# Projection weights and a weight remainder moved from the SyncE load queue to the ScalarE load queue, with a staging buffer

## The chip, the cores and the metric

The kernel runs on one core of one Trainium2 chip. The metric is device time in microseconds (us), the median over several executions. Ratios are the mean time of one kernel's runs over the mean of the other's in the same rounds, so they are not quite the ratio of the medians that are quoted.

## The reference, cut to what matters

The program adds three things: the input `x` (8 rows of 640), an attention block over a key and value cache, and a small MLP. Attention has 8 batch rows, 32 heads, 4096 cached positions and a head size of 128, in bfloat16.

```python
xn = layernorm(x)
q = xn @ wq                                    # wq 640 x 4096
p = softmax(q . k_cache / sqrt(128))           # k_cache 8 x 32 x 4096 x 128
o = p . v_cache                                # v_cache the same size
out = x + o @ wo + mlp(xn)                     # wo 4096 x 640; mlp: w1 640 x 1728, w2 1728 x 640
```

K and V together are 537 MB (8 x 32 x 4096 x 128 elements, 2 bytes, twice), read once. The weights are 15 MB: wq and wo 5.2 MB each, w1 and w2 2.2 MB each.

## The kernel before

The work is cut into 64 tiles. A tile is one batch row and a "quad" of four heads: 4 MB of K (32 KB in each of 128 partitions) and 4 MB of V. Eight tiles make a quad, and each quad needs its own 0.66 MB slice of `wo`. There are two K buffers and two V buffers. Each operation carries a position; operations of one engine run in order of position, and waits follow from what they read (`R`) and write (`W`). Tile `t` has its scores near position `t`, its values near `t + 2`. Repeated windows of operations become hardware loops.

All large loads are issued by SyncE, which does nothing else, in one queue:

```python
def ld(pos, dst, src, W, sem, R=()):
    add("sp", pos, lambda e: e.dma_start(dst, src() if callable(src) else src), R=R, W=W, sem=sem)
...
# K of tile t at t - 1.5, V of tile t at t + 0.6 (the first two of each earlier)
ld(-95.1, w2_sb[:, 0:FC, :], ..., ["w2"], "w2")
ld(-95.0, w2_sb[0:FR, FC, :], B_w2[FC * P:F, :], ["w2r"], "w2r")
for hg in range(NG):                                # NG = 8 quads, B = 8 tiles each
    ld(hg * B + 3.65, wo_sb[:, :, :],
       lambda hg=hg: A_wo[span(hg, HT * P), :].rearrange("(a p) n -> p a n", p=P), ["wo"], "wo")
```

The projection of the previous quad's last pair of tiles reads `wo_sb` at position 3.33 of the quad, so the load at 3.65 has to wait for it, and every K and V load behind it in the queue waits as well:

```python
def pe_o(e):
    for a in range(HT):
        for c in range(DC):
            r = e.matmul(ACC_ps[:, c * B:(c + 1) * B], wo_sb[:, a, c * P:(c + 1) * P], oTn_sb[:, a, :], ...)
add("pe", g * GT + 5.33 ..., pe_o, R=["wo", "oTn"], W=["ACC"], X=["ACC"], sig=True)
```

VectorE computes three quarters of the scores (a product, an add, a reduction, twice per tile, 17 us in all); TensorE does the other quarter and the value sums.

## Time and profile before

| | before |
|---|---|
| time, median of 3 | 1293.12 us (1292.88 to 1293.37) |
| moved by DMA | 552.00 MB |
| VectorE / TensorE / ScalarE busy | 1122.2 / 640.8 / 497.1 us of 1291.2 |

Parts 2 and 3 of the page of the kernel before: the mean busy share of the 16 DMA engines and their rate, in 40 slices of 32.3 us, and the queue that SyncE issues on, with packets, MB and share of 16 engines' span.

```profile
DMA  9999999999999999999999999999999999999997
GB/s 407 423 427 427 435 429 431 433 429 427 434 430 431 428 434 427 434 431 427 430 434 430 432 427 431 430 434 430 427 432 431 431 433 428 429 432 430 429 435 329
q1 hardware_dynamic: 23472, 551.80, 99.7%
```

The engines that move data are busy for 90% or more of every slice but the last. The DMA part of the page of the same kernel gives for each load the count, the size and the median time from issue to landing:

```profile
KV_sb<-in_A_k_cache_dram SPq DMA_DIRECT2D x64, 4096.0 KB, 26.8
KV_sb<-in_A_v_cache_dram SPq DMA_DIRECT2D x63, 4096.0 KB, 35.2
wo_sb<-in_A_wo_dram SPq DMA_DIRECT2D x8, 640.0 KB, 30.9
```

At 431 GB/s, 4 MB take 9.7 us. A load that lands 27 to 35 us after its issue has therefore stood behind two or three others: there is a backlog. The waits of the SyncE queue itself, in the kernel before (who, on whom: us in total, times, longest):

```profile
SPq L178 <- DVE Y_sb L544: 948.9, 56, 20.7
SPq L365 <- PE PV_ps L616: 75.6, 50, 20.8
SPq L365 <- PE ACC_ps L676: 43.5, 8, 6.2
```

The first two are waits for a K or V buffer to come free, the normal way in which consumers pace a full stream. The third is what the change is aimed at: 43.5 us in which the queue stood before the eight wo loads. Last, three links of the chain that ended last (start, length, what), before:

```profile
247.17 35.06 DMA KV_sb<-in_A_v_cache_dram
285.91 36.95 DMA KV_sb<-in_A_v_cache_dram
326.54 35.17 DMA KV_sb<-in_A_v_cache_dram
```

A link is one V load from issue to landing. The landings are at 282.23, 322.86 and 361.71 us. Two tiles of K and V lie between two of them: 38.85 us without a wo load, 40.63 us with one. So a wo load costs some 1.77 us of the stream.

VectorE's costliest group before (busy, mean ns of one, idle just before it and what ended it) shows that VectorE waits for data:

```profile
L544 DVE TENSOR_TENSOR Y_sb<-KV_sb,qbc_sb 128x6144 bf16<-128x6144 bf16 x128 | 429.1, 3353 | 91.0 <-DMA KV_sb<-in_A_k_cache_dram 76.4
```

### The profile page before, as it was taken

The page shows a single profiled execution, that of the slowest core. Times are in us where ns is not written, and L with a number is a line of the kernel's source. Part 1 is how long each engine was busy: PE and PEld are TensorE (multiplying, and loading weights), DVE is VectorE, ACT ScalarE, POOL GpSimd, SP SyncE. Part 2 cuts the span into 40 slices and gives each one's busy share as a digit, 9 for nine tenths or more (in the row PEclk, how much of TensorE's full clock was granted, in tenths as well). Part 3 has the DMA queues.
Part 4 walks back from the last instruction along what each step waited for, and adds up shares of the span by engine and source line. Part 5 has one row for each costly group of instructions (what it writes and reads, how often), then busy time and mean ns, then how long its engine had stood idle before and what let it go on. Part 6 is the DMA issues. An engine that isn't in the chain of part 4 may idle for free.

```text
span 1291.2 us, 19910 instructions
## 1 busy us (share of the span) xinstructions
PE 640.8 (50%) x7958; PEld 406.5 (31%) x7960; DVE 1122.2 (87%) x586; ACT 497.1 (39%) x1244; POOL 0.2 (0%) x4
## 2 busy tenths in 40 slices
PE   2754455444554454454455445545544554544555
PEld 1433233323333233233233233333332332322332
DVE  4989999898898898898988988988888988889885
ACT  1444344324344334344244342343442443433442
POOL 0000000000000000000000000000000000000000
PEclk9755655565555565655655555555555655556556
DMA  9999999999999999999999999999999999999997
GB/s 407 423 427 427 435 429 431 433 429 427 434 430 431 428 434 427 434 431 427 430 434 430 432 427 431 430 434 430 427 432 431 431 433 428 429 432 430 429 435 329
DMA packets 23520, 552.00 MB, mean 428 GB/s; under 512 B 2297, under 2 KB 6481, under 8 KB 6482
## 3 DMA queue, kind: packets, MB, share of 16 engines
q1 hardware_dynamic: 23472, 551.80, 99.7%
q8 instruction: 8, 0.13, 0.0%
q14 instruction: 6, 0.05, 0.0%
q10 hardware_dynamic: 34, 0.02, 0.0%
HBM read 551.80 MB, written 0.01 MB: 427 GB/s over the span
## 4 chain that ended last, share of the span: by engine, by line
DMA 83%; PE 8%; DVE 7%; issue 2%; ACT 0%; SPq 0%; DVEq 0%
DMA KV_sb<-in_A_v_cache_dram 78%; PE PV_ps L616 8%; DVE Y_sb L544 4%; DMA KV_sb<-in_A_k_cache_dram 2%; DMA KV_sb<-in_A_wq_dram 2%; DVE Y_sb L548 2%; DVE S_sb L551 1%; SPq L365 0%; PE PV_ps L626 0%; DVE M_sb L563 0%; PE CH_ps L565 0%; PE TR_ps L665 0%; PE TR_ps L456 0%; PE CH_ps L478 0%; DVE rinv_sb L597 0%
## 5 line engine op out<-in xcount | busy, mean ns | idle before, releaser
L544 DVE TENSOR_TENSOR Y_sb<-KV_sb,qbc_sb 128x6144 bf16<-128x6144 bf16 x128 | 429.1, 3353 | 91.0 <-DMA KV_sb<-in_A_k_cache_dram 76.4
L551 DVE TENSOR_REDUCE S_sb<-Y_sb 128x48 f32<-128x3072 bf16 x128 | 429.2, 3353 | 4.4
L515 ACT ACTIVATE KT_sb<-TR_ps 128x1024 bf16<-128x1024 bf16 x256 | 254.6, 1021 | 229.2 <-PE TR_ps L512 227.8
L616 PE MATMUL PV_ps<-KV_sb,P_sb 128*16 128x512 bf16 x2040 | 223.1, 616 | 144.2 <-DMA KV_sb<-in_A_v_cache_dram 144.2
L512 PE MATMUL TR_ps<-ident_bf,KV_sb 128*128 128x128 bf16 x2048 | 248.4, 308 | 74.7 <-DMA KV_sb<-in_A_k_cache_dram 74.7
L548 DVE TENSOR_TENSOR Y_sb<-Y_sb 128x3072 bf16<-128x3072 bf16 x128 | 225.0, 1758 | 4.4
L512 PEld LDWEIGHTS TR_ps<-ident_bf,KV_sb 128*128 128x128 bf16 x2048 | 200.4, 141 | 85.1 <-DMA KV_sb<-in_A_k_cache_dram 79.3
L522 PE MATMUL S_ps<-qk_sb,KT_sb 128*128 128x4 bf16 x2048 | 98.0, 170 | 135.7 <-ACT KT_sb L515 133.9
L635 ACT ACTIVATE E_sb<-PV_ps 128x512 bf16<-128x512 f32 (+1 forms) x65 | 38.5, 592 | 320.7 <-PE PV_ps L616 318.8
L616 PEld LDWEIGHTS PV_ps<-KV_sb,P_sb 128*16 128x16 bf16 x2040 | 62.5, 124 | 256.9 <-DMA KV_sb<-in_A_v_cache_dram 149.6
L522 PEld LDWEIGHTS S_ps<-qk_sb,KT_sb 128*128 128x128 bf16 x2048 | 85.9, 109 | 167.1 <-ACT KT_sb L515 167.1
L583 ACT ACTIVATE P_sb<-S_sb,NB_sb 32x128 bf16<-32x128 f32 x256 | 101.9, 398 | 3.8
L641 PE MATMUL C_ps<-sel_bf,E_sb 128*128 128x4 bf16 x256 | 16.9, 172 | 137.9 <-DVE rinv_sb L597 114.8
L577 ACT ACTIVATE NB_sb<-CH_ps 128x2 f32<-128x2 f32 (+1 forms) x33 | 5.7, 172 | 171.1 <-PE CH_ps L573 171.1
L565 PE MATMUL CH_ps<-ident_f,M_sb 128*2 128x128 f32 (+1 forms) x33 | 12.1, 366 | 114.1 <-DVE M_sb L563 114.1
L641 PEld LDWEIGHTS C_ps<-sel_bf,E_sb 128*128 128x128 bf16 x256 | 11.4, 103 | 167.9 <-DVE rinv_sb L597 114.1
L532 ACT ACTIVATE S_sb<-S_ps 32x32 f32<-32x32 f32 x256 | 48.3, 189 | 32.0 <-PE S_ps L522 29.8
L583 ACT ACTIVATION_READ_ACCUMULATOR P_sb<-S_sb,NB_sb 32x1 f32 x256 | 47.1, 184 | 0.0
L565 PEld LDWEIGHTS CH_ps<-ident_f,M_sb 128*2 128x2 f32 (+1 forms) x33 | 2.6, 80 | 117.1 <-DVE M_sb L563 117.1
L656 DVE MEMSET oTn_sb<- 128x16 uint32 x31 | 2.2, 72 | 31.1 <-PE ACC_ps L676 31.1
L567 DVE TENSOR_REDUCE M_sb<-CH_ps 2x4 f32<-2x128 f32 (+1 forms) x33 | 9.2, 279 | 15.1 <-PE CH_ps L565 15.1
L676 PE MATMUL ACC_ps<-oTn_sb,wo_sb 128*128 128x8 bf16 x620 | 21.5, 169 | 0.0
(93 smaller groups left out, 196.1 us busy)
## 6 DMA issues: line engine op xcount, KB each, us to landing
KV_sb<-in_A_k_cache_dram SPq DMA_DIRECT2D x64, 4096.0 KB, 26.8
KV_sb<-in_A_v_cache_dram SPq DMA_DIRECT2D x63, 4096.0 KB, 35.2
KV_sb<-in_A_wq_dram SPq DMA_DIRECT2D x1, 5120.0 KB, 24.0
wo_sb<-in_A_wo_dram SPq DMA_DIRECT2D x8, 640.0 KB, 30.9
KV_sb<-in_B_w_dram SPq DMA_DIRECT2D x1, 2160.0 KB, 39.2
w_sb<-in_B_w_dram SPq DMA_DIRECT2D x1, 2080.0 KB, 43.8
KV_sb<-in_A_v_cache_dram SPq DMA_DIRECT2D x1, 2048.0 KB, 12.6
KV_sb<-in_A_v_cache_dram SPq DMA_DIRECT2D x2, 1024.0 KB, 15.3
```

Of the source, the lines that this page charges most:

```text
L512: r = e.transpose(TR_ps[:, it.box[0], jj * P:(jj + 1) * P], kv[:, n * BK + jj, :], ident_bf[:, :])
L515: add("act", t - 0.59 + 0.12 * n, lambda e: e.activation(KT_sb[:, m % NS, :, :].rearrange("p a b -> p (a b)"), TR_ps[:, it.box[0], :], ACT ...
L522: r = e.matmul(S_ps[:, c:c + HT], KT_sb[:, m % NS, jj, :], qk_sb[:, :, i], start=True, stop=True)
L532: r = e.activation(S_sb[s, g % SR, i, 0:JP], S_ps[s, 0:JP * HT].rearrange("p (j a) -> p j a", a=HT)[:, :, a], ACT.Copy)
L544: return e.tensor_tensor(y, kv[:, j0:j1, :], qbc_sb[:, g % 2, i, :][:, None, :].to_broadcast([P, nj, P]), ALU.mult)
L548: lambda e, y=y, y2=y2: e.tensor_tensor(y2, y[:, :, 0:P // 2], y[:, :, P // 2:P], ALU.add),
L551: lambda e, y2=y2, j0=j0, j1=j1: e.tensor_reduce(S_sb[:, g % SR, i, j0:j1], y2, AX.X, ALU.add),
L583: r = e.activation(P_sb[s, i, :, a, :], S_sb[s, g % SR, i, :].rearrange("p (m c) -> p m c", c=4), ACT.Exp, bias=NB_sb[s, g % 2, i:i + 1], ...
L616: r = e.matmul(PV_ps[32 * ct:32 * ct + HT * 4, t % 2, :], P_sb[:, i, m, :, :].rearrange("p a c -> p (a c)"), vv[:, 4 * m:4 * m + 4, :].rea ...
L635: add("act", pos, lambda e: e.activation(E_sb[:, k, 0:n], PV_ps[:, k, 0:n], ACT.Copy), R=[("PV", k)] + ["wo"] * (t % GT), W=[("E", k)], X= ...
L641: r = e.matmul(OT_i, E_sb[:, t % 2, c * P:(c + 1) * P], sel_bf[:, c:HT * 4:4], start=(c == 0), stop=(c == 3 and not last))
L676: r = e.matmul(ACC_ps[:, c * B:(c + 1) * B], wo_sb[:, a, c * P:(c + 1) * P], oTn_sb[:, a, :], start=False, stop=False, skip_group_check=True)
```

## The change

The intent is to free the load queue. wo goes through the ScalarE queue, one quad ahead of its use, into a staging buffer, so that nothing has to wait for the old wo to be read; when it has been read, VectorE copies the new one over. The last 64 rows of w2 also move to the ScalarE queue, at the start.

```diff
+        wost_sb = sb("wost_sb", [P, HT, D], BF)
-        ld(-95.0, w2_sb[0:FR, FC, :], B_w2[FC * P:F, :], ["w2r"], "w2r")
+        add("act", -99.7, lambda e: e.dma_start(w2_sb[0:FR, FC, :], B_w2[FC * P:F, :]), W=["w2r"], sem="w2r")
+        def wo_load(hg):
+            add("act", hg * B - 3.0 if hg else 1.05, lambda e: e.dma_start(
+                wost_sb[:, :, :], A_wo[span(hg, HT * P), :].rearrange("(a p) n -> p a n", p=P)), W=["wost"], sem="wo")
+            add("dve", hg * B + 3.37, lambda e: e.tensor_copy(wo_sb[:, :, :], wost_sb[:, :, :]), R=["wost"], W=["wo"])
         for hg in range(NG):
-            ld(hg * B + 3.65, wo_sb[:, :, :], ..., ["wo"], "wo")
+            wo_load(hg)
 ...
-                    R=[("PV", k)] + ["wo"] * (t % GT), W=[("E", k)], X=[("PVb", k)])
+                    R=[("PV", k)], W=[("E", k)], X=[("PVb", k)])
 ...
-                R=["OT", ("rinv", g % 2), "oTn0"], W=["oTn"], X=["C2"])
+                R=["OT", ("rinv", g % 2), "oTn0"] + ["wost"] * (g % GPH == 0), W=["oTn"], X=["C2"])
```

More of the change, by code (lines that the diff above doesn't have):

```diff
@@ L393, in bass_parallel_sum__gqa_block_cached__mixer_channel_mlp__decode_kernel @@
         ld(-95.1, w2_sb[:, 0:FC, :], B_w2[0:FC * P, :].rearrange("(k c) n -> k c n", c=FC), ["w2"], "w2")
-        ld(-95.0, w2_sb[0:FR, FC, :], B_w2[FC * P:F, :], ["w2r"], "w2r")
+        add("act", -99.7, lambda e: e.dma_start(w2_sb[0:FR, FC, :], B_w2[FC * P:F, :]), W=["w2r"], sem="w2r")
[3 more added lines that the diff above has]
+            add("dve", hg * B + 3.37, lambda e: e.tensor_copy(wo_sb[:, :, :], wost_sb[:, :, :]), R=["wost"], W=["wo"])
         for hg in range(NG):
-            ld(hg * B + 3.65, wo_sb[:, :, :],
-               lambda hg=hg: A_wo[span(hg, HT * P), :].rearrange("(a p) n -> p a n", p=P), ["wo"],
-               "wo")
+            wo_load(hg)
         def layernorm(n, pos, src, src_res, dst, dst_res):
```

## The prediction

> **What bounds the kernel now.** The DMA engines. The page's DMA row has 9 in 39 of 40 slices, and the queue section gives q1 99.7% of 16 engines' span: 551.80 MB in 1291.2 us. The windows view shows a steady 431 GB/s from 180 to 1180 us. The chain of waits is 83% DMA, 78% V tiles. VectorE is 87% busy but waits for K (76.4 us before its products); it is second.
>
> **How deep the stream is.** The DMA section shows 26.8 us (K), 35.2 us (V) and 30.9 us (wo) from issue to landing, while 4 MB take 9.7 us at 431 GB/s: two to three transfers are always queued. The queue's own waits show what the change is aimed at: before the 8 wo loads the queue stands 43.5 us in all (longest 6.2) until the projection has read the old wo. But wo still takes at least 21.3 us to land after that: the backlog never ran dry. This head-of-line wait is real and costs nothing.
>
> **What wo costs in the stream.** In the chain, V landings two tiles apart are 38.9 us apart, and 40.6 us with a wo load between: 1.77 us for 0.655 MB, against 1.52 us at 431 GB/s. Its 512 rows of 1280 B lose about 0.25 us each time, 2 us over eight loads.
>
> **What changes.** No byte is removed: eight wo loads (5.2 MB) and the w2 remainder (80 KB) move to the ScalarE queue. The Trainium skill, "DMA: Bandwidth & Descriptors", section "Issuing engines are not separate DMA queues", says such DMAs interleave on the same 16 engines; I expect the trace to agree. Removed: the 43.5 us of queue waits (worth 0). Added: eight issues on ScalarE (0.38 us each on the SP queue; ScalarE is 39% busy), and eight VectorE copies of 128x2560. The add of 3072 columns takes 1.76 us, so a copy takes at most 1.5 us; "VectorE: DVE Perf Modes", section "The perf-mode tier table", gives a bf16 copy twice the rate of a two-tensor operation, so I estimate 0.75 us, 6 us in all. VectorE has some 170 us of slack: 0 on the critical path.
>
> **Size.** Interleaving 1280 B packets with the 32 KB packets of K and V could hide part of the 2 us, or pay for switching (8 loads x 32 small packets per engine = 256 switches each way[...]). I expect these nearly to cancel. Start (wq landing near 25 us) and tail (last V piece to the end, 5 us) stay.
>
> Predicted time: 1292.3 us, 80% range 1287 to 1299. Chances: faster by over 2% 0.01, within 2% 0.96, slower by over 2% 0.03.
>
> **What would show each step right.** DMA total still 552.0 MB, share above 99%, 429 to 432 GB/s in the middle. The queue's waits for the projection line vanish, and its waits for the buffers (VectorE products, PV matmuls) grow by about as much. K and V landing times stay, or grow by a few us. wo takes longer to land, some 40 us, because each small packet alternates with a 32 KB one of 1.2 us. VectorE busy rises by about 6 us.
>
> **What would make it wrong.** If switching queues costs each engine a bubble, the mid-run rate falls below 425 GB/s and the time rises towards 1305. If the first wo load, issued near 55 us, lands after about 105 us, VectorE stalls early, where the chain runs through it; the backlog should absorb that. If the middle rate rises above 433 GB/s, mixing the rows helps and I was too pessimistic.

## The result, and the profile after

| | before | after |
|---|---|---|
| time, median of 6 | 1293.11 us (1292.65 to 1293.37) | 1293.27 us (1293.09 to 1293.31) |
| ratio, 95% interval | | 1.0002, 0.9989 to 1.0014 |
| VectorE busy | 1122.2 us | 1128.6 us |
| rate from 180 to 1180 us | 431 GB/s | 431 GB/s |

The time is the same. The page of the changed kernel, parts 2 and 3 (q10 is the queue that ScalarE issues on):

```profile
DMA  9999999999999999999999999999999999999997
GB/s 394 429 433 425 432 431 428 434 428 433 428 434 430 432 427 434 428 434 430 429 429 434 431 427 431 432 429 435 428 431 431 432 429 432 430 431 432 432 431 331
q1 hardware_dynamic: 19168, 546.47, 98.5%
q10 hardware_dynamic: 4338, 5.35, 1.2%
```

5.3 MB changed queues, and the sum of the two shares is what one queue had before: 99.7%. This is what the Trainium skill, "DMA: Bandwidth & Descriptors", section "Issuing engines are not separate DMA queues", says: the loads of all issuers run on the same 16 engines. The DMA part of the changed kernel's page:

```profile
KV_sb<-in_A_k_cache_dram SPq DMA_DIRECT2D x64, 4096.0 KB, 26.8
KV_sb<-in_A_v_cache_dram SPq DMA_DIRECT2D x63, 4096.0 KB, 35.2
wost_sb<-in_A_wo_dram ACTq DMA_DIRECT2D x8, 640.0 KB, 42.2
```

K and V have the same medians as before. wo takes 42.2 us, not 30.9. The section "Queues, rings and completion order" of the same page says that an engine takes turns between queues packet by packet. The trace lists a wo load as 512 packets, one for each row of 1280 B, so 32 per engine. If each waits for one 32 KB packet of K or V (1.22 us in the trace), that makes 39 us, an estimate. The measured 42.2 us agrees, and so does the spread of the packets: those of the second quad start from 284.7 to 321.6 us, where before they started from 279.5 to 283.4. (The page's own packet is typically 9 to 17 descriptors; in this trace the turns come row by row.) The waits of SyncE's queue in the changed kernel:

```profile
SPq L178 <- DVE Y_sb L549: 989.7, 56, 20.5
SPq L366 <- PE PV_ps L621: 74.8, 46, 19.3
```

The wait for the projection is gone from the list. The wait for K buffers grew by 40.8 us, nearly all of the 43.5 us that went: the queue now stands as long, one entry later. The chain after, at the same place as before:

```profile
249.19 35.03 DMA KV_sb<-in_A_v_cache_dram
287.90 37.00 DMA KV_sb<-in_A_v_cache_dram
328.58 35.18 DMA KV_sb<-in_A_v_cache_dram
```

The landings are 40.68 us apart with a wo load between (284.22 to 324.90) and 38.86 us without: unchanged. The copies are new, and VectorE's idle time before its product shrinks from 91.0 to 83.7 us. The lines are the copies (durations in ns, least, median and most) and the product's group:

```profile
L401 DVE COPY wo_sb<-wost_sb x8: 826/827/828, 107.0 to 1198.6; 128x2560 bf16<-128x2560 bf16 x8
L549 DVE TENSOR_TENSOR Y_sb<-KV_sb,qbc_sb 128x6144 bf16<-128x6144 bf16 x128 | 429.1, 3352 | 83.7 <-DMA KV_sb<-in_A_k_cache_dram 68.3
```

VectorE paid for the 6.6 us of copies out of time in which it would have waited for K.

### The profile page after: what moved, and what is told of

Read it like the earlier page. It is cut to its first block, busy times and chain, and to the rows that moved or that the text cites. A ratio compares the mean times of both kernels' runs of the same rounds, so it can differ in the third digit from the quotient of the medians.

```text
span 1291.4 us, 19913 instructions
## 1 busy us (share of the span) xinstructions
PE 648.7 (50%) x7958; PEld 409.3 (32%) x7960; DVE 1128.6 (87%) x594; ACT 497.1 (38%) x1244; POOL 0.2 (0%) x4
## 4 chain that ended last, share of the span: by engine, by line
DMA 80%; DVE 9%; PE 8%; issue 3%; ACT 0%; SPq 0%; DVEq 0%
DMA KV_sb<-in_A_v_cache_dram 76%; PE PV_ps L621 7%; DVE Y_sb L549 5%; DMA KV_sb<-in_A_k_cache_dram 2%; DVE Y_sb L553 2%; DMA KV_sb<-in_A_wq_dram 2%; DVE S_sb L556 2%; DVE M_sb L568 0%; SPq L366 0%; PE CH_ps L570 0%; PE PV_ps L631 0%; PE TR_ps L670 0%; PE TR_ps L461 0%; PE ACC_ps L681 0%; DVE rinv_sb L602 0%
## 5 line engine op out<-in xcount | busy, mean ns | idle before, releaser
L549 DVE TENSOR_TENSOR Y_sb<-KV_sb,qbc_sb 128x6144 bf16<-128x6144 bf16 x128 | 429.1, 3352 | 83.7 <-DMA KV_sb<-in_A_k_cache_dram 68.3
L621 PE MATMUL PV_ps<-KV_sb,P_sb 128*16 128x512 bf16 x2040 | 226.5, 623 | 137.0 <-DMA KV_sb<-in_A_v_cache_dram 137.0
L553 DVE TENSOR_TENSOR Y_sb<-Y_sb 128x3072 bf16<-128x3072 bf16 x128 | 225.0, 1758 | 4.4
L599 PEld LDWEIGHTS C_ps<-rs_sb,ones_f 128*128 128x128 f32 x64 | 14.0, 273 | 25.0 <-issue 13.8
## 6 DMA issues: line engine op xcount, KB each, us to landing
KV_sb<-in_A_k_cache_dram SPq DMA_DIRECT2D x64, 4096.0 KB, 26.8
KV_sb<-in_A_v_cache_dram SPq DMA_DIRECT2D x63, 4096.0 KB, 35.2
KV_sb<-in_A_wq_dram SPq DMA_DIRECT2D x1, 5120.0 KB, 24.8
wost_sb<-in_A_wo_dram ACTq DMA_DIRECT2D x8, 640.0 KB, 42.2
```

The costliest lines, as they stand in the source:

```text
L549: return e.tensor_tensor(y, kv[:, j0:j1, :], qbc_sb[:, g % 2, i, :][:, None, :].to_broadcast([P, nj, P]), ALU.mult)
L553: lambda e, y=y, y2=y2: e.tensor_tensor(y2, y[:, :, 0:P // 2], y[:, :, P // 2:P], ALU.add),
L621: r = e.matmul(PV_ps[32 * ct:32 * ct + HT * 4, t % 2, :], P_sb[:, i, m, :, :].rearrange("p a c -> p (a c)"), vv[:, 4 * m:4 * m + 4, :].rea ...
```

## The experiments

"Nothing gained" leaves three readings. Theory A: the stream is full all the time, so the queue waits never cost anything, and neither do the copies. Rival B: the waits did cost something, and the copies or the second queue took it back. Rival C: the two halves of the change cancel each other. All runs but one were timed over three rounds; the kernel before ran on the same chip beside each group, at 1292.96, 1293.02 and 1293.10 us.

### Taking out seven wo loads with their waits

```diff
-        for hg in range(NG):
+        for hg in range(1):
             ld(hg * B + 3.65, wo_sb[:, :, :], ...
```

> The kernel before with seven of its eight wo loads, and their queue waits, taken out (wrong result on purpose). Theory A, the stream is full and waits are free: 7 x 1.77 us of transfer go, 12.4 us, so about 1280.7 us (1279 to 1282.5). Rival B, the queue waits for the projection cost time which something in the changed kernel gave back: part of their 7/8 of 43.5 us goes too, so clearly below 1278 us.

Measured: 1280.94 us, ratio 0.9906 (0.9889 to 0.9922). That is 12.02 us less, 1.72 us for each load, as theory A has it. The comparison of outputs still passed although seven slices of wo were stale; its tolerance doesn't see this part of the sum.

### The same loads in longer rows

```diff
-               lambda hg=hg: A_wo[...].rearrange("(a p) n -> p a n", p=P), ["wo"],
+               lambda hg=hg: A_wo[...].rearrange("(p a) n -> p a n", p=P), ["wo"],
```

> The kernel before with wo loaded in rows of 5120 B instead of 1280 B (wrong result on purpose, same bytes, same place in the queue). If small rows are what makes a wo load cost 1.77 us instead of 1.52, then 2 us less, about 1291.1 us, and the V landing gap with a wo load falls from 40.6 to 40.4 us. If rows of this size cost nothing extra: 1293.1 us and 40.6 us.

Measured: 1291.23 us, ratio 0.9985 (0.9969 to 1.0002). The interval touches 1, so the time alone doesn't settle it, but the trace agrees with the expectation. The link with a wo load, in this kernel's chain:

```profile
285.34 37.08 DMA KV_sb<-in_A_v_cache_dram
```

The landing at 322.42 us is 40.42 us after the previous one (282.00), against 40.63 before.

### One half of the change at a time

The w2 remainder alone:

```diff
-        ld(-95.0, w2_sb[0:FR, FC, :], B_w2[FC * P:F, :], ["w2r"], "w2r")
+        add("act", -99.7, lambda e: e.dma_start(w2_sb[0:FR, FC, :], B_w2[FC * P:F, :]), W=["w2r"], sem="w2r")
```

> The kernel before with only the w2 remainder moved to the ScalarE queue. Theory A: no change, 1293.1 us within 1.5, with wq landing 0.5 to 1 us later as in the changed kernel. Rival C, the two halves of the change cancel: a loss of 2 us or more here and a gain in the other half.

Measured: 1293.00 us, ratio 0.9998 (0.9981 to 1.0015). wq takes 24.7 us to land instead of 24.0, as in the changed kernel (24.8). Then the wo part alone, which is the changed kernel with this line put back:

> The changed kernel with the w2 remainder put back on the SP queue; the wo loads stay on the ScalarE queue with staging and copy. Theory A: no change, 1293.1 us within 1.5. Rival C: a gain of 2 us or more here that the other half takes back.

Measured: 1292.98 us, ratio 0.9999 (0.9982 to 1.0016). Neither half does anything that can be told from zero, so rival C falls.

### A longer wait in the queue

These two kernels make the old queue wait worse. K of tile 5 and V of tile 3 of each quad are moved behind the wo load, so the queue reaches its wait for the projection earlier and has more behind it; the second kernel also moves V of tile 2.

```diff
             pos = (-100.0, -98.0)[t] if t < NK else t - 1.5
+            if t % B == 5:
+                pos = t - 1.34
 ...
             pos = (0.45, 1.2)[t] if t < NV else t + 0.6
+            if t % B == 3:                                   # first kernel
+                pos = t + 0.67
+            if t % B in (2, 3):                              # second kernel, instead
+                pos = t // B * B + (3.652 if t % B == 2 else 3.67)
```

> The kernel before with one K and one V load moved behind the wo load, so the queue stands longer for the projection, some 7 us, with two big loads behind it; the backlog at that point is some 19 us. Theory A: 1293 us within 2. Rival B, queue waits cost time: the larger wait shows, 8 x 2 to 7 us more, 1309 us or higher.

Measured: 1296.44 us, ratio 1.0026 (1.0009 to 1.0043); more than my 2 us, far less than rival B's.

> The same with a second V load behind the wo load: the queue stands some 25 us, against a backlog of 26 to 28 us. Theory A: at the edge, 0 to 2 us lost per quad, 1293 to 1308 us, and the smallest time to landing of wo falls to a few us. Rival B: 8 x 20 us more or a good part of it, above 1350 us.

Measured: 1324.29 us, ratio 1.0241 (1.0223 to 1.0258); 31 us, twice my upper figure, still far from rival B's. The windows view shows where each loses. Columns: stretch in us, its length, busy time of TensorE, its weight loads, VectorE, ScalarE and GpSimd, then granted clock, DMA share and GB/s. The kernel before, in the first quad and in the second:

```profile
80.00:120.00 40.00, 19.05 (x239) 12.46 (x239) 35.72 (x18) 15.25 (x38) 0.00 (x0) 0.56 1.01 432
240.00:280.00 40.00, 18.82 (x242) 11.84 (x239) 35.81 (x18) 15.89 (x42) 0.00 (x0) 0.59 0.99 427
```

The kernel with two loads behind the wait, first quad:

```profile
80.00:120.00 40.00, 19.27 (x239) 12.36 (x239) 35.73 (x18) 15.23 (x38) 0.00 (x0) 0.53 0.94 397
```

The kernel with three, first and second quad:

```profile
80.00:120.00 40.00, 15.33 (x205) 10.99 (x205) 35.71 (x19) 14.65 (x37) 0.00 (x0) 0.52 0.67 281
240.00:280.00 40.00, 17.17 (x219) 11.71 (x211) 35.82 (x18) 15.25 (x38) 0.00 (x0) 0.54 0.93 392
```

The wait of SyncE's queue for the projection, with two loads behind it and with three:

```profile
SPq L365 <- PE ACC_ps L680: 199.3, 8, 25.6
SPq L365 <- PE ACC_ps L680: 209.1, 8, 26.4
```

With two loads behind it, the first quad runs at 397 instead of 432 GB/s for 40 us, a loss of 3.2 us, which is the whole difference of 3.4. The queue's waits for the projection rose from 43.5 to 199.3 us in that kernel (25.6 us in the first quad and 25.1 in the second, not the 7 I had expected: I had overlooked that the wait starts as soon as the load ahead of it is issued). Still, in the seven later quads the added waiting cost nothing: summed over the windows, the bytes moved lag behind the kernel before by the same 3 us at 120, 600 and 1240 us. With three loads behind it, the wait is hardly longer (26.2 and 26.1 us), but one 4 MB load less, 9.7 us of transfer, has been issued ahead of it: the first quad loses 14 us and each later one some 2.5 us. What is left of the backlog shows in the time that wo itself takes to land after the wait. In the second quad it is 30.9 us before, 11.6 with two loads behind, and 4.2 with three. In the first quad it is 4.1 us in both of the edited kernels. Some 4 us is thus what wo takes with little or nothing left ahead of it. In these runs a wait costs only what it exceeds the backlog by. The backlog of the first quad is smaller: already in the kernel before, wo landed 21.3 us after its issue there and 31 us later on.

### More of the same loads, on either queue

Fourteen more wo-sized loads into a scratch buffer nobody reads, on one queue or the other (the ScalarE version also waits for the last of them at its end). On the SyncE queue they stand at places where they wait for no projection.

```diff
+            for off in (-0.4, 2.2) if hg else ():
+                add("sp", hg * B + off, lambda e, hg=hg: e.dma_start(        # "act" in the other kernel
+                    wox_sb[:, :, :], A_wo[span(hg, HT * P), :].rearrange("(a p) n -> p a n", p=P)), W=["wox"], sem="wox")
```

> The kernel before with 14 more wo-sized loads into a scratch buffer on the SP queue. Each should cost what a wo load costs in the stream, 1.72 to 1.77 us: 24 to 25 us more, about 1317.5 us.

Measured: 1318.35 us, ratio 1.0196 (1.0179 to 1.0213): 25.25 us for 14 loads, 1.80 us each.

> The changed kernel with the same 14 loads on the ScalarE queue. If interleaving small packets with large ones costs nothing and hides nothing: the same 24 to 25 us more, about 1317.5 us. If it hides the loss of small rows: 21 us, about 1314.5 us or less. If switching queues has a price: clearly more than 25 us.

Measured: 1319.42 us, ratio 1.0202 (1.0185 to 1.0219). Against the changed kernel's 1293.27, which was timed in an earlier group, this is 26.15 us, 1.87 us each. Most of the two ratios' intervals overlap. Mixing 1280 B packets with 32 KB packets on two queues neither hid the loss of small rows nor had a price that can be told from zero.

The SyncE figure also decides against rival B. A load without a projection wait costs 1.80 us; one of the original loads, with its wait of 5.4 us (43.5 over 8), cost 1.72 us. If the waits cost time, the second figure would be the larger. By the intervals of the two ratios the first is 1.65 to 1.97 us and the second 1.44 to 2.05, so at most 0.4 us of each 5.4 us wait could have cost time. Part 3 of the page before gives a bound of its own: the packets took 99.7% of the span, so all idle time of the engines, start and tail included, is some 4 us.

### More copies

The changed kernel with every copy done ten or thirty times:

```diff
             add("dve", hg * B + 3.37, lambda e: e.tensor_copy(wo_sb[:, :, :], wost_sb[:, :, :]), R=["wost"], W=["wo"])
+            for n in range(9):                                # 29 in the other kernel
+                add("dve", hg * B + 3.3701 + 0.0001 * n, lambda e: e.tensor_copy(wo_sb[:, :, :], wost_sb[:, :, :]),
+                    R=["wost", "wo"], W=["wo"])
```

> The changed kernel with each wo copy done ten times: about 8 us more VectorE work per quad of heads, 60 to 67 us in all. Theory A, VectorE has slack and the backlog covers it: 1293 us within 2. Rival B, the copies stand on the path and their 6.6 us are what the removed queue waits were paid back with: some 60 us more, about 1353 us.

Measured: 1306.20 us, ratio 1.0099 (1.0083 to 1.0116). I had said no change within 2 us. VectorE's busy time rose by 57 us (1128.6 to 1185.2), so most was free, but 13 us were not. (Some 10 of the 13 came in with another side effect of the edit, shown in the next part.)

> The same with thirty copies, some 26 us more per quad of 8 tiles. VectorE then needs about 137 + 27 + 6 = 170 us per quad against 156 us of transfer, so it becomes the bound: theory A expects 8 x 6 to 14 us more, 1340 to 1400 us, and gaps in the DMA row. If it stayed at 1293 us, the reading of VectorE's slack would be wrong.

Measured: 1420.17 us, one run, state unknown; above my range. VectorE is busy 1315.9 us here, and the rate in part 2 of its page drops once per quad:

```profile
GB/s 401 430 428 219 379 434 431 429 256 436 424 432 433 262 428 432 428 430 263 429 431 431 430 262 429 429 429 404 287 432 432 431 332 360 426 430 434 277 418 283
```

So VectorE does become the bound when it is given enough, at a place I had put too far away.

### The two sides of the change apart, and a confounder

One kernel adds the copy (into a scratch buffer) and keeps wo on the SyncE queue with its waits:

```diff
+            add("dve", hg * B + 3.37, lambda e: e.tensor_copy(wox_sb[:, :, :], wo_sb[:, :, :]), R=["wo"], W=["wox"])
```

> The kernel before, wo still loaded on the SP queue with its waits, plus eight VectorE copies of wo into a scratch buffer at the place where the changed kernel copies. It has the added cost of the change without its removed waits. Theory A: one copy of 0.83 us per quad is free, 1293.1 us within 1.5. Rival B: 6.6 us or a part of it, 1296 to 1300 us.

Measured: 1303.10 us, ratio 1.0077 (1.0060 to 1.0094), 10 us more. The other takes the waits away and adds no copy: wo goes through the ScalarE queue at the old place, straight into `wo_sb`.

```diff
-            ld(hg * B + 3.65, wo_sb[:, :, :], ..., ["wo"], "wo")
+            add("act", hg * B + 3.65, lambda e, hg=hg: e.dma_start(
+                wo_sb[:, :, :], A_wo[span(hg, HT * P), :].rearrange("(a p) n -> p a n", p=P)), W=["wo"], sem="wo")
 ...
-                    R=[("PV", k)] + ["wo"] * (t % GT), W=[("E", k)], X=[("PVb", k)])
+                    R=[("PV", k)], W=[("E", k)], X=[("PVb", k)])
```

> The kernel before with wo loaded through the ScalarE queue straight into wo_sb at the old place, no staging and no copy: the queue waits are gone without their price. Theory A: no gain, 1293.1 us within 1.5 after the first quad; as wo takes some 42 us to land on this queue and is needed about 35 us after its issue, the projection waits some 7 us per quad, and in the thin first quad that may lose up to 3 us. Rival B: up to several us faster, 1288 us or below.

Measured: 1303.77 us, ratio 1.0086 (1.0069 to 1.0103), 10.7 us more. Both expectations failed, by the same amount and for two quite different edits. What they have in common is in part 3 of the page. The kernel before:

```profile
q8 instruction: 8, 0.13, 0.0%
```

The kernel with the copy alone:

```profile
q1 hardware_dynamic: 23472, 551.80, 99.0%
q8 instruction: 58, 0.95, 0.3%
```

Queue q8 fetches instructions. My edits changed which operations wait for which, so the windows of TensorE's program no longer had equal waits, and the emitter, which rolls only equal windows into a loop, left most of that program as straight code: it has 7385 instructions instead of 1040. The same line, 58 packets, stands in the pages of the two kernels with many copies; it is 8 packets in every other kernel here. The packets are 16 KB each, as the Trainium skill, "Runtime: NRT & Kernel Launch", section "Instruction fetch mechanics", gives for one refill, and they go through the same DMA engines as the data.

The loss builds up steadily. Two V links of the chain, in the kernel before and then in the kernel with the copy alone, the same tiles in both:

```profile
600.36 37.00 DMA KV_sb<-in_A_v_cache_dram
...
1229.53 36.91 DMA KV_sb<-in_A_v_cache_dram
```

```profile
605.14 36.89 DMA KV_sb<-in_A_v_cache_dram
...
1238.63 38.48 DMA KV_sb<-in_A_v_cache_dram
```

The landing is late by 4.7 us halfway (642.03 against 637.36) and by 10.7 us at the end (1277.11 against 1266.44). The bytes moved, summed over the windows, lag by only 3.0 us at 1240 us, or 4.8 us if the 0.8 MB of fetched instructions are taken out. And just before the later of these V loads is complete, the engines no longer have enough to do. The windows view from 1272 to 1280 us, before and with the copy alone:

```profile
1272.00:1280.00 8.00, 4.77 (x51) 1.57 (x49) 2.49 (x5) 2.42 (x10) 0.00 (x0) 0.79 0.95 407
```

```profile
1272.00:1280.00 8.00, 2.86 (x29) 0.98 (x32) 7.93 (x4) 0.75 (x4) 0.00 (x0) 0.50 0.63 270
```

The mean DMA share is 0.63 there while two V loads are still landing and the next can't be issued before the first of them is used. A reading that fits all three is that the fetches load some of the 16 engines more than the others: a load is complete when its slowest engine is, so landings fall behind further than bytes do, and at the end the faster engines run dry.

The views give only the engines' mean, but the packets of the packed trace can be counted: with the copy alone, 16 are under way at every full microsecond from 1252 to 1273 us and exactly 8 from 1276 to 1280, where the kernel before has 16 or more up to 1283. So half of the engines had run ahead of the other half. From 243 us on the landings of V, each set against the same one before, fall behind in seven steps of some 1.6 us (0.0, 1.6, 3.1, 4.7, 6.2, 7.8, 9.3, 10.7 us), one in about 159 us, the time of eight fetches. A fetch packet takes some 1.06 us, and a data packet of twice its bytes 1.22 us. That some engines fall behind the others is thus shown. That the fetches are what holds up the slower half is argued from the steps: the trace doesn't name the engine of a packet, and no run adds fetches alone. What the runs show is the correlation: 58 packets in four kernels, each some 10 us or more slower, where the bytes themselves are worth 1.9 us at 431 GB/s.

The pairs within that group can still be compared. Without waits and without copies: 1303.77 us, though the projection there waits for wo (64.2 us in all, 8 times). With waits and one copy each: 1303.10. Without waits and with ten copies each: 1306.20. So 62 us of added VectorE work (9 x 8 x 0.86 us, start to start) cost some 3 us, which is not clear of noise (the intervals of the two ratios overlap). The windows show where; from 120 to 160 us, the kernel before and then the one with ten copies:

```profile
120.00:160.00 40.00, 19.77 (x253) 13.23 (x254) 38.07 (x20) 15.24 (x38) 0.00 (x0) 0.59 1.01 432
```

```profile
120.00:160.00 40.00, 14.79 (x197) 10.60 (x197) 38.03 (x19) 13.61 (x33) 0.00 (x0) 0.57 0.91 382
```

That is 4.6 us of transfer lost right after the first quad's copies, the same thin first quad as above. I made no clean pair, with a rolled TensorE program, for the copy alone and for the missing wait alone, so those two are settled by the loads' costs above and by the wo half alone (copies without waits, 1292.98 us), not by these runs.

## Why the prediction was right

The predicted 1292.3 us and the range 1287 to 1299 hold the measured 1293.27. The 0.8 us that it lies below the kernel before is less than these runs can tell, so only "no change" was tested. Point by point:

- **The stream is the bound, and its backlog swallows the queue waits.** Right. The 43.5 us went from one line of the queue's waits to another (948.9 to 989.7), K and V landings stayed at 26.8 and 35.2 us, and the cost per load with a wait (1.72 us) is not above that without (1.80 us). That the backlog "never ran dry" was true, but it was said without telling how near it came: in the first quad a wait of 26 us instead of 6.2 loses 3 us or 14 us, depending on how many loads were issued ahead of it.
- **wo costs 1.77 us each, 0.25 of it for small rows.** Right: 1.72 us by removal, 1.80 by addition, and 0.21 us less in the trace with 5120 B rows.
- **Copies are free.** Right for the eight copies of the change. The estimate of 0.75 us for one was a little low: 0.827 us, and 6.4 us more busy time. The prediction took the copy's rate as twice the add's, from the page that it names; here a column took 0.323 ns in the copy (2560 columns) and 0.572 ns in the add (3072 columns in 1758 ns), 1.77 times. The reason given, 170 us of slack, was too coarse: an average over the run. In the first quad the chain runs through VectorE, and there ten copies did lose transfer time.
- **Interleaving hides and costs about as much.** It does neither that can be told: 1.87 us per load on the second queue, 1.80 on the first.
- **wo lands after some 40 us.** Right, 42.2, and it was issued at 54 us and needed at 107, so nothing waited for it.
- **The start stays.** Not quite: wq landed 0.9 us later (26.02 against 25.15 us), because the w2 remainder now travels early, beside K and wq. It cost nothing, as the run with that half alone shows (wq lands at 25.91 us, 1293.00 us in all).

## What to carry to other kernels

When a load queue stands waiting, look at how long its loads take from issue to landing before paying for its removal: in this kernel the waits were covered, and only bytes counted, as long as the loads already issued took longer than the wait. A second issuing engine added no bandwidth to the full stream (431 GB/s on one queue and on two). And when an experiment in a kernel with rolled loops gives a surprise, compare the instruction-fetch lines first: a changed dependency can unroll another engine's program, which came with 10 us here, in edits that by theory A were worth little or nothing.

## What the Trainium skill lacked or had wrong

- "Runtime: NRT & Kernel Launch", section "Instruction fetch mechanics", calls the cost of crossing a 16 KiB boundary "mostly hidden", and its remark on branches prefers full unrolling. It doesn't say that beside a full data stream the fetches compete for the DMA engines: the four kernels with 58 fetch packets (0.95 MB) instead of 8 were some 10 us or more slower, of which the bytes explain 1.9 us; the rest is put down to the fetches by argument, as said above.
- "DMA: Bandwidth & Descriptors", section "Why small descriptors are slow (HBM only)", deems joining descriptors into packets worth it only up to 256 B, and has no figure for rows that are themselves longer, which is what was tried here. 5120 B instead of 1280 B rows shortened a landing gap by 0.21 us, some 9 ns for each of 24 packets saved per engine. The time, 1.7 us of 1293, was within noise.
- "DMA: Bandwidth & Descriptors", section "Queues, rings and completion order", gives the packet-by-packet turns between queues, with 9 to 17 descriptors as typical for a packet, but not what follows for latency; here the turns came row by row, and a load of small rows beside a queue of 32 KB packets took 42.2 us to land instead of 30.9 us in the common queue.
- No page says how much backlog a wait on the load queue may use up; here 25 us were free in seven quads of eight with two loads behind the wait, and 26 us were not with three.
